# One tensor per chunk of tokens for the attention output, a third buffer for the reciprocals' rows, and a regrouped weight split

## The chip, the cores and the metric

The kernel runs on one core of a Trainium2 chip. The metric is the device time of one execution, in microseconds (us). Times of other kernels are set against it on the same chip.

## The reference, cut to what matters

The program is a chain of three layers over B·S = 2·768 = 1536 tokens of 512 features.

```python
# 1. attention of 8 heads of 64 features, with keys masked by equality of hash buckets
scores = np.where(mask, scale * q @ k.T, -1e9); attn = softmax(scores)   # sums + 1e-9
x = attn @ v                      # -> x: 1536 x 512
# 2. a gated dense layer
a = x @ w1; b = x @ w2            # 512 -> 1024 each
x = ((a * b) @ w3) @ w_out        # 1024 -> 1024 -> 512
# 3. a mixture of 8 experts, one per token, chosen by argmax of x @ w_gate + bias
out[mask] = gate_w * (np.maximum(x[mask] @ e1[e], 0) @ e2[e])
```

## The kernel before

**Storage.** The unnormalised attention output stands transposed, features on partitions: 512 features are four groups `hp` of 128 (two heads each), and tokens run along the free axis. There is one tensor for each of the two batches, `xT[b]` of `[P, HP, S + 1]` with S = 768; its last column holds a sum that is used for tokens without a matching key. The tokens are worked on in four chunks of CH = 384: chunks 0 and 1 are the halves of `xT[0]`, chunks 2 and 3 those of `xT[1]`.

**Splitting.** Matmuls take float32 numbers as a rounded high part and a remainder, in three products for each (`TERMS`: high·high, high·low, low·high). For the activations the high part is `x_t[ch]`, a tensor of its own, and the remainder `xlo` is written in place over the memory of `xT`.

**Normalisation of a chunk.** The attention output of each token and head is divided by its sum. The reciprocals come from DRAM (`rd`), spread over 64 partitions for each head by `load_r`, into the ring of buffers `rb`, two transfers for one `hp`. For chunks 1 to 3 `norm_step(ch, step)` starts one `hp` at each step: DVE makes `nw`, POOL multiplies `xT` by `rb` (L648) and adds `nw` (L649), ACT rounds it into `x_t` a step later (L651), and DVE writes the remainder a step after that (L653). Chunk 0 is normalised during attention, by DVE alone, in `norm_0`.

**The dense layer of a chunk.** `moe_f(ch, f)` computes 128 of the 1024 features in two tiles, `a` (j = 0) and `b` (j = 1), of 12 matmuls each (L686). ACT copies `a` to `asb` (L689), DVE multiplies it with `b` into `gf` (L696), ACT rounds that into `g` (L697), POOL subtracts the remainder (L698). In this phase the tiles turn over four PSUM buffers. The first four `f` of chunk 0 are worked in between the last attention steps, the last four after them.

**What runs when.** The order of the instructions on each engine is the order in which the code is written out. While chunk 0 does its `f` = 4 to 7, the steps of `norm_step(1, ·)` are issued, two ahead of each `moe_f`; while chunks 1 and 2 do `f` = 2 to 7, one step of the next chunk's normalisation follows each `moe_f`. The matrix products with `w3 @ w_out` (called w34; tiles `x2p`, L1022) of a chunk follow `f` = 3 of the next. `w34_prep` splits w34 in eight blocks at the start of chunk 1: ACT copies a block (L674), DVE subtracts (L675); the loaded w34 (`w34f`) shares its memory with the remainders. Waits between engines follow from the tensors that instructions touch: where two tensors lie on the same memory, as `xlo` on `xT`, a reader of the one is held by the last earlier writer of the other, whichever part it wrote.

**Transfers.** All loads named here are issued by SP, in the order of the code; an issue whose wait is open holds those behind it.

Of the kernel before, what the change touches and what calls it, by code (L numbers as in the profile page):

```python
# [8 lines left out]
F32 = mybir.dt.float32  # L9
# [11 lines left out]
P = 128  # L21
# [148 lines left out]
def body(tc, qT, kT, vP, w1d, w2d, w3d, wod, mod, wgate, mbias, e1, e2, cst, out):  # L170
# [6 lines left out]
    def one(name, shape, dt=F32, at_top=False):  # L177
        n = 4
        for d in shape[1:]:
            n *= d  # L180
        rings[name] = Ring(mem, name, n, 1, at_top)
        return rings[name](shape, dt)

    def ring(name, words, n, at_top=False, below=None):
        return Ring(mem, name, 4 * words, n, at_top, below)
# [26 lines left out]
    mv = one("mv", [P, B, HP])  # L212
    logit = one("logit", [P, TT, E])
    wgs = one("wgs", [P, 4, 32])
    mbs = one("mbs", [P, 2, E])
    mods = one("mods", [P, 2 * TT], I32)
    wgp = one("wgp", [P, 8, 32])
    xT = {b: one(f"xT{b}", [P, HP, S + 1]) for b in range(B)}

    rg = {"rb": ring("rb", CH, 2, True), "nw": ring("nw", CH, 1, True)}  # L220
    r_raw = ring("raw", S, 6, True)
    r_bt = ring("bt", S, 1, True)
    r_lo = ring("lo", S, 1, True)
# [164 lines left out]
    def stage_a(j):  # L388
        p, half, c = sunits[j]
        v = v_t[p]  # L390
        if c == 0:
            a_t[p, half] = ps("a", [P, HS + 1], f"a{p}_{half}")
        for hd in range(2):
            PE.matmul(  # L394
                a_t[p, half][64 * hd:64 * hd + 64, :], v[:, c, 64 * hd:64 * hd + 64], pts[j % NP][:, hd, :],
                start=(c == 0), stop=(c == QT - 1), tile_position=(0, 64 * hd),
            )
        if c == QT - 1:
            b, hp = divmod(p, HP)
            o = half * HS  # L400
            ACT.copy(xT[b][:, hp, o:o + HS + 1], a_t.pop((p, half)))

    def stage_n(p):
        b, hp = divmod(p, HP)
        sm = ps("m", [P, HS], f"n{p}")
        for half in range(2):
            acc = acc_t.pop((p, half))
            for hd in range(2):
                r = 64 * half + 32 * hd
                PE.matmul(  # L410
                    sm[r:r + 32, :], cs[:, 416:448], acc[:, hd, 0:HS], start=True, stop=True, tile_position=(0, r),
                )
        ss = r_ss([P, HS])
        ACT.copy(ss, sm)  # L414
        for half in range(2):
            SP.dma_start(sd[b, :, hp, half * HS:half * HS + HS], ss[64 * half:64 * half + 64:32, :])
        if hp == HP - 1:
            sm, r, z = (r_sr([P, 48]) for _ in range(3))
            SP.dma_start(sm, sd[b].rearrange("j h (a n) -> (j h a) n", n=48))

            def recip():
                DVE.tensor_scalar(r, sm, 1e-9, None, ALU.add)
                DVE.reciprocal(r, r)
                DVE.tensor_scalar(z, sm, 0.0, -4e9, ALU.is_equal, ALU.mult)
                DVE.tensor_add(r, r, z)
                SP.dma_start(rd[b].rearrange("j h (a n) -> (j h a) n", n=48), r)
                DVE.tensor_scalar(mv[:, b, :], xT[b][:, :, S], 1.0 / S, None, ALU.mult)

            late.append(recip)

# [204 lines left out]
        for j in range(2):  # L635
            SP.dma_start(rb_t[ch, hp][64 * j:64 * j + 64], rd[b, j, hp, o:o + CH].partition_broadcast(64))

    xlo = {b: mem.at(rings[f"xT{b}"].spans[0], [P, HP, S + 1], F32R, f"xlo{b}") for b in range(B)}

    def norm_x(ch, hp, part):  # L640
        b, o = divmod(ch * CH, S)
        if part and ch not in x_t:
            x_t[ch] = rg["x"]([P, HP, CH], F32R)
        x = xT[b][:, hp, o:o + CH]
        if part == 0:
            w = rg["nw"]([P, CH])
            DVE.tensor_scalar(w, rb_t[ch, hp], 0.0, mv[:, b, hp:hp + 1], ALU.is_lt, ALU.mult)
            POOL.tensor_mul(x, x, rb_t[ch, hp])  # L648
            POOL.tensor_add(x, x, w)  # L649
        elif part == 1:  # L650
            ACT.copy(x_t[ch][:, hp, :], x)  # L651
        else:
            DVE.tensor_sub(xlo[b][:, hp, o:o + CH], x, x_t[ch][:, hp, :].bitcast(F32))  # L653

    def norm_0(ch, hp, s):
        b, o = divmod(ch * CH, S)
        x = xT[b][:, hp, o:o + CH]
        if s == 0:
            DVE.tensor_mul(x, x, rb_t[ch, hp])
        elif s == 1:  # L660
            nw_t[ch, hp] = rg["nw"]([P, CH])
            DVE.tensor_scalar(nw_t[ch, hp], rb_t[ch, hp], 0.0, mv[:, b, hp:hp + 1], ALU.is_lt, ALU.mult)
        else:
            DVE.tensor_add(x, x, nw_t.pop((ch, hp)))
# [5 lines left out]

    TERMS = ((0, 0), (0, 1), (1, 0))

    def w34_prep(f):
        ACT.copy(w34[0][:, f, :], w34[2][:, f, :])  # L674
        DVE.tensor_sub(w34[1][:, f, :], w34[2][:, f, :], w34[0][:, f, :].bitcast(F32))  # L675

    ab_t, gspan = {}, []

    def moe_half(ch, f, j, tag="ab"):
        b, o = divmod(ch * CH, S)  # L680
        x = (x_t[ch], xlo[b][:, :, o:o + CH])
        fs = slice(f * P, f * P + P)
        t = ps(tag, [P, DM], f"ab{ch}{f}{j}")[:, 0:CH]
        for c in range(4):
            for i, (st, mv) in enumerate(TERMS):
                PE.matmul(t, w12[j][:, st, c, fs], x[mv][:, c, :], start=(c == 0 and i == 0), stop=(c == 3 and i == 2))  # L686
        if j == 0:
            ab_t[ch, f] = rg["asb"]([P, CH])
            ACT.copy(ab_t[ch, f], t)  # L689
            return  # L690
        if f % 4 == 0:
            gf_t[ch, f // 4] = rg["gf"]([P, 4, CH])
            g_t[ch, f // 4] = mem.at(gspan[GSPAN[ch][f // 4]], [P, 2, 4, CH], F32R, "g")
        gf = gf_t[ch, f // 4][:, f % 4, :]
        g = g_t[ch, f // 4][:, :, f % 4, :]
        DVE.tensor_mul(gf, ab_t.pop((ch, f)), t)  # L696
        ACT.copy(g[:, 0, :], gf)  # L697
        POOL.tensor_sub(g[:, 1, :], gf, g[:, 0, :].bitcast(F32))  # L698
# [91 lines left out]
    for i in range(NU + LEAD + NLAG + 1):  # L790
# [31 lines left out]
            norm_step(0, i - SWITCH - NSTEP)  # L822
        for ch, at in enumerate(NORM):
            for hp in range(HP):
                if i == at + (0, 0, 8, 11)[hp]:
                    load_r(ch, hp)
            if i == at + 4:
                for k in range(12):
                    after(k, lambda ch=ch, k=k: norm_0(ch, k // 3, k % 3))
# [8 lines left out]
        if done["n"] == 56 and len(rg["gf"].spans) == 1:  # L838
            r_st.close()
            rg["gf"].grow(1, 4 * 4 * CH)  # L840
            rg["rb"].grow(2, 4 * CH)
        p, ph = divmod(i, 12)
        j = i - LEAD + (i < SOON)
        both = grouped(i)
# [124 lines left out]
    load_r(1, 3)  # L969
    for f in range(0, 8, 2):  # L970
        SP.dma_start(w34[2][:, f:f + 2, :], w34d[f * P:(f + 2) * P, :].rearrange("(f p) n -> p f n", p=P))
    SP.dma_start(mbs, mbias.rearrange("m e -> (m e)").partition_broadcast(P))
    SP.dma_start(mods.bitcast(I64), mod)

# [61 lines left out]

    for ch in range(NCH):
        if ch == NCH - 1:
            rings["xT0"].close()
            gspan.append(mem.take(4 * 2 * 4 * CH))  # L1040
        for f in range(NEARLY if ch == 0 else 0, 8):
            if ch == 0:
                for step in range(2 * (f - NEARLY), 2 * (f - NEARLY) + 2):
                    norm_step(1, step)
            if ch == 1 and f < 3:
                for k in range(3 * f, min(8, 3 * f + 3)):
                    w34_prep(k)
            moe_f(ch, f)
            if f == 5:
                logit_mm(ch, 0)  # L1050
            if ch == 0 and f == 6:
                late.pop(0)()
            if ch and f == 1:
                logit_mm(ch - 1, 1)
                logit_evac(ch - 1)
            if ch and f == 2:
                logit_fin(ch - 1)
            if ch and ch + 1 < NCH:
                if f < HP:
                    load_r(ch + 1, f)  # L1060
                if 0 <= f - 2 < HP + 2:
                    norm_step(ch + 1, f - 2)
            if ch and f == 3:
                for tile in range(TC * (ch - 1), TC * ch - (ch == NCH - 1)):
                    for it in x2_items(tile):
                        it()
        if ch == 1:
            mf, mn = (one(n, [P, TT]) for n in ("mf", "mn"))
            b0, b1 = (one(n, [P, TT, E]) for n in ("b0", "b1"))
            DVE.tensor_copy(mf, mods.rearrange("p (t two) -> p t two", two=2)[:, :, 0])  # L1070
            DVE.tensor_scalar(mn, mf, -1.0, 1.0, ALU.mult, ALU.add)
            DVE.tensor_mul(b0, bc(mbs[:, 0, :], 1, TT), bc(mn, 2, E))
            DVE.tensor_mul(b1, bc(mbs[:, 1, :], 1, TT), bc(mf, 2, E))
            DVE.tensor_add(b0, b0, b1)
    for n in ("x", "rb", "nw", "asb"):
        rg[n].close()
    for n in ("xT1", "w0", "w1"):
        rings[n].close()
    xi = [it for tile in range(TT - 4, TT) for it in x2_items(tile)]
    for it in xi[:HOOKS[0]]:  # L1080
# [468 lines left out]
```

## Time and profile before

| | |
|---|---|
| time, median of 3 runs (lowest to highest) | 708.34 us (706.29 to 709.06) |
| profiled execution: its time | 704.57 us |
| profiled execution: span from first to last instruction | 702.2 us |
| mean granted TensorE clock | 0.983 |
| PE busy | 653.6 us, 93% of the span |
| DVE / ACT / POOL busy | 383.0 / 319.3 / 320.8 us |

The page and the views come from one execution. Durations are read from it; 2.4 us of its time lie outside the span, and its time is 0.5% below the median of the three runs. "Granted clock" 1.00 is TensorE's upper level (2.4 GHz), 0.50 the lower one (1.2 GHz). In a row, "[3.27 <-POOL xT L649]" says that the engine stood idle for 3.27 us before it and that the POOL instruction of line 649, which writes `xT`, ended that.

### The profile page before, as it was taken

How to read it: one execution, taken by the hardware profiler on the slowest of the kernel's cores; microseconds unless marked ns; L12 is line 12 of the kernel's file. 1: busy time of each engine (PE TensorE's matmuls, PEld its weight loads, DVE VectorE, ACT ScalarE, POOL GpSimd, SP SyncE). 2: the span in 40 equal slices, each digit the busy share in tenths (PEclk: the TensorE clock that was granted, in tenths of full speed). 3: DMA queues.
4: the chain of work that ended last, by engine and by line, in shares of the span. 5: the costliest groups of instructions: out<-in, count | busy, mean ns of one | idle time of the engine just before them, and what ended most of it. 6: DMA issues, size and time to landing. Idle time of an engine off the chain costs nothing. (4 is left out here: it accounts for less than half of the span.)

```text
span 702.2 us, 10151 instructions
## 1 busy us (share of the span) xinstructions
PE 653.6 (93%) x3650; PEld 516.7 (74%) x3650; DVE 383.0 (55%) x573; ACT 319.3 (45%) x510; POOL 320.8 (46%) x291
## 2 busy tenths in 40 slices
PE   7988999999999989976999979699999999999996
PEld 2644756666666645855998978598978998899884
DVE  6798777676867887521432311120176675665560
ACT  7466565656566447531332211121213665555551
POOL 7698986877778677752241330321114232011101
PEclk9999999999999999997999999899999999999999
DMA  8748372737565672203102001000007887766630
GB/s 228 232 136 224 101 245 86 230 114 191 178 166 175 165 214 79 100 25 121 48 15 64 12 0 46 0 1 16 16 17 257 291 297 237 233 208 215 210 136 18
DMA packets 40663, 93.88 MB, mean 134 GB/s; under 512 B 6544, under 2 KB 11008, under 8 KB 40608
## 3 DMA queue, kind: packets, MB, share of 16 engines
q1 hardware_dynamic: 38528, 86.62, 39.6%
q0 software_dynamic: 2080, 6.56, 2.8%
q8 instruction: 31, 0.51, 0.3%
q14 instruction: 24, 0.20, 0.1%
HBM read 72.98 MB, written 12.94 MB: 122 GB/s over the span
## 5 line engine op out<-in xcount | busy, mean ns | idle before, releaser
L686 PE MATMUL ab<-x,w 128*128 128x384 f32 x512 | 141.8, 353 | 0.6 <-ACT ss L414 0.6
L386 POOL TENSOR_TENSOR acc<-acc,pt 128x770 f32<-128x770 f32 x64 | 119.9, 1874 | 23.6 <-ACT pt L381 22.1
L356 DVE TENSOR_REDUCE nm<-m 128x1 f32<-128x768 f32 x96 | 91.4, 955 | 51.2 <-PE m L348 51.0
L381 ACT ACTIVATE pt<-s 128x768 f32<-128x768 f32 x96 | 77.9, 812 | 73.5 <-PE s L380 67.9
L686 PE MATMUL ab<-xlo,w 128*128 128x384 f32 x256 | 90.1, 352 | 20.6 <-POOL xT L649 20.6
L698 POOL TENSOR_TENSOR g<-gf,g 128x384 fp32r<-128x384 f32 x32 | 32.6, 1017 | 154.9 <-ACT g L697 153.6
L686 PEld LDWEIGHTS ab<-x,w 128*128 128x128 f32 x512 | 98.7, 199 | 5.8 <-issue 3.8
L380 PE MATMUL s<-q,k 128*128 128x384 f32 (+1 forms) x384 | 91.0, 359 | 4.0 <-ACT pt L381 3.9
L380 PEld LDWEIGHTS s<-q,k 128*128 128x128 f32 (+1 forms) x384 | 63.6, 189 | 38.7 <-issue 15.0
L1213 DVE TENSOR_TENSOR eu<-er,eu 128x1024 fp32r<-128x1024 f32 x56 | 67.6, 1223 | 23.7 <-ACT eu L1212 22.6
L696 DVE TENSOR_TENSOR gf<-asb,ab 128x384 f32<-128x384 f32 x32 | 17.7, 553 | 113.0 <-PE ab L686 113.0
L394 PE MATMUL a<-pt,v 128*64 128x385 f32 x384 | 74.5, 502 | 0.0
L1378 PE MATMUL e1F<-ex,eu 128*128 128x256 f32 x576 | 70.4, 283 | 0.5 <-DVE ex L1342 0.3
L1378 PEld LDWEIGHTS e1F<-ex,eu 128*128 128x128 f32 x576 | 69.9, 192 | 1.3 <-DVE ex L1342 0.5
L1404 POOL DMA_INDIRECT out<-o,sidx x13 | 14.2, 1095 | 122.3 <-ACT o L1403 106.2
L1396 PE MATMUL e2F<-eu,h 128*128 128x512 f32 x288 | 68.1, 392 | 0.0
L686 PEld LDWEIGHTS ab<-xlo,w 128*128 128x128 f32 x256 | 50.9, 199 | 22.1 <-POOL xT L649 22.0
L1212 ACT CAST eu<-er 128x1024 fp32r<-128x1024 f32 x56 | 57.6, 1047 | 8.8 <-DMA er<-e 8.8
L1396 PEld LDWEIGHTS e2F<-eu,h 128*128 128x128 f32 x288 | 53.2, 188 | 10.6
L348 PE MATMUL m<-k,q 78*128 78x384 f32 x192 | 52.5, 355 | 5.9 <-ACT pt L381 2.5
L1022 PE MATMUL x2p<-w,g 128*128 128x512 f32 x240 | 56.0, 391 | 0.0
L1022 PEld LDWEIGHTS x2p<-w,g 128*128 128x128 f32 x240 | 44.8, 188 | 9.6 <-issue 0.6
(207 smaller groups left out, 870.2 us busy)
## 6 DMA issues: line engine op xcount, KB each, us to landing
er<-e SPq DMA_DIRECT2D x56, 512.0 KB
cr<-w3d SPq DMA_DIRECT2D x16, 512.0 KB
cr<-wod SPq DMA_DIRECT2D x8, 512.0 KB
cr<-w1d SPq DMA_DIRECT2D x8, 512.0 KB
wfd<-cT SPq DMA_DIRECT2D x16, 256.0 KB
cr<-w2d SPq DMA_DIRECT2D x8, 512.0 KB
st<-wfd SPq DMA_DIRECT2D x16, 256.0 KB
raw<-kT SPq DMA_DIRECT2D x8, 384.0 KB
```

Of the source, the lines that this page charges most:

```text
L348: PE.matmul(s[:, half, 0:HS], q[0:KROWS[hd], 0, qt * P:qt * P + P], k[0:KROWS[hd], 0, half * HS:half * HS + HS], start=True, stop=True,)
L356: DVE.tensor_reduce(nm[:, at:at + 1], s[:, :, 0:HS], AX.XY, ALU.max, negate=True)
L380: PE.matmul(s[:, hd, 0:HS], k[0:n, i, c * P:c * P + P], q[0:n, i, cl], start=(i == 0), stop=(i == 1))
L381: ACT.activation(pts[j % NP][:, :, 0:HS], s[:, :, 0:HS], AF.Exp, scale=SCALE)
L386: POOL.tensor_add(acc, pts[(j - 1) % NP] if c == 1 else acc, pts[j % NP])
L394: PE.matmul(a_t[p, half][64 * hd:64 * hd + 64, :], v[:, c, 64 * hd:64 * hd + 64], pts[j % NP][:, hd, :], start=(c == 0), stop=(c == QT - 1 ...
L686: PE.matmul(t, w12[j][:, st, c, fs], x[mv][:, c, :], start=(c == 0 and i == 0), stop=(c == 3 and i == 2))
L1022: PE.matmul(st["ps"], g_t[ch, f // 4][:, a, f % 4, i * P:i * P + P], w34[b][:, f, :], start=(f == 0 and k == 0), stop=(f == 7 and k == 2),)
L1212: ACT.copy(t[:, 0, sl], raw)
L1213: DVE.tensor_sub(t[:, 1, sl], raw, t[:, 0, sl].bitcast(F32))
L1378: PE.matmul(o[f], w[:, st, c, fs], x[:, mv, c, :], start=(c == 0 and i == 0), stop=(c == 3 and i == 2))
L1396: PE.matmul(o, h[:, st, f, sl], w[:, mv, f, :], start=(f == 0 and k == 0), stop=(f == 7 and k == 2))
```

## The change

The attention output is kept in four tensors `xT[ch]` of `[P, HP, CH + 1]`, one for each chunk, and `xlo` in four over them. The ring `rb` has three buffers from the start in place of two, and four after it grows, as before; the loads of `hp` 2 and 3 of chunk 0 are issued eight and three slots earlier. `w34_prep` takes a group of blocks, copies all of it and then subtracts all of it. `mbs` and `mods`, two small tables, get their memory later in the program; their loads stay at their place.

```diff
-    mbs = one("mbs", [P, 2, E])
-    mods = one("mods", [P, 2 * TT], I32)
...
-    xT = {b: one(f"xT{b}", [P, HP, S + 1]) for b in range(B)}
-
-    rg = {"rb": ring("rb", CH, 2, True), "nw": ring("nw", CH, 1, True)}
+    xT = [one(f"xT{ch}", [P, HP, CH + 1]) for ch in range(NCH)]
+
+    rg = {"rb": ring("rb", CH, 3, True), "nw": ring("nw", CH, 1, True)}
...
-            o = half * HS
-            ACT.copy(xT[b][:, hp, o:o + HS + 1], a_t.pop((p, half)))
+            ACT.copy(xT[2 * b + half][:, hp, :], a_t.pop((p, half)))
...
-    xlo = {b: mem.at(rings[f"xT{b}"].spans[0], [P, HP, S + 1], F32R, f"xlo{b}") for b in range(B)}
+    xlo = [mem.at(rings[f"xT{ch}"].spans[0], [P, HP, CH + 1], F32R, f"xlo{ch}") for ch in range(NCH)]
...
-        x = xT[b][:, hp, o:o + CH]
+        x = xT[ch][:, hp, 0:CH]
...
-            DVE.tensor_sub(xlo[b][:, hp, o:o + CH], x, x_t[ch][:, hp, :].bitcast(F32))
+            DVE.tensor_sub(xlo[ch][:, hp, 0:CH], x, x_t[ch][:, hp, :].bitcast(F32))
...
-    def w34_prep(f):
-        ACT.copy(w34[0][:, f, :], w34[2][:, f, :])
-        DVE.tensor_sub(w34[1][:, f, :], w34[2][:, f, :], w34[0][:, f, :].bitcast(F32))
+    def w34_prep(fs):
+        for f in fs:
+            ACT.copy(w34[0][:, f, :], w34[2][:, f, :])
+        for f in fs:
+            DVE.tensor_sub(w34[1][:, f, :], w34[2][:, f, :], w34[0][:, f, :].bitcast(F32))
...
-        x = (x_t[ch], xlo[b][:, :, o:o + CH])
+        x = (x_t[ch], xlo[ch][:, :, 0:CH])
...
-                if i == at + (0, 0, 8, 11)[hp]:
+                if i == at + (0, 0, 0, 8)[hp]:
                     load_r(ch, hp)
...
-            rg["rb"].grow(2, 4 * CH)
+            rg["rb"].grow(1, 4 * CH)
+            rg["rb"].i = 7
...
+    mbs = one("mbs", [P, 2, E])
+    mods = one("mods", [P, 2 * TT], I32)
     SP.dma_start(mbs, mbias.rearrange("m e -> (m e)").partition_broadcast(P))
...
-            rings["xT0"].close()
+            for n in ("xT0", "xT1"):
+                rings[n].close()
...
-                for k in range(3 * f, min(8, 3 * f + 3)):
-                    w34_prep(k)
+                w34_prep(range(3 * f, min(8, 3 * f + 3)))
...
-    for n in ("xT1", "w0", "w1"):
+    for n in ("xT2", "xT3", "w0", "w1"):
```

The order of instructions on PE, DVE, ACT and POOL is the same before and after; on SP one pair of loads moves. What changes on the four engines is which instructions wait, and on whom. A row below is one instruction (or xN alike): its line, operation, what it writes and reads, its shape, and the engines or transfers that it waits for.

PE, at the first tile after attention, `ab040` (chunk 0, `f` = 4, j = 0); `x_` is the high part, `xlo0` the remainder. Before:

```order
L686 MATMUL ab040_2936<-x_223_2554,w0_220_2500 128x384 [waits Activation_49]
L686 MATMUL ab040_2936<-xlo0_27_96,w0_220_2500 128x384 [waits Pool_49]
L686 MATMUL ab040_2936<-x_223_2554,w0_220_2500 128x384 x2
L686 MATMUL ab040_2936<-xlo0_27_96,w0_220_2500 128x384
L686 MATMUL ab040_2936<-x_223_2554,w0_220_2500 128x384 x2
```

After:

```order
L684 MATMUL ab040_2940<-x_225_2556,w0_222_2502 128x384 [waits Activation_49]
L684 MATMUL ab040_2940<-xlo0_27_96,w0_222_2502 128x384
L684 MATMUL ab040_2940<-x_225_2556,w0_222_2502 128x384 x2
L684 MATMUL ab040_2940<-xlo0_27_96,w0_222_2502 128x384
L684 MATMUL ab040_2940<-x_225_2556,w0_222_2502 128x384 x2
```

The second matmul waits for POOL before and for nobody after. The same wait goes from the tiles `ab050`, `ab230`, `ab240`, `ab250` and `ab260`.

PE, at the first tile of chunk 1 (`ab100`), which reads the remainders `xlo1` in the kernel after. Before:

```order
L686 MATMUL ab100_3094<-xlo0_27_96,w0_220_2500 128x384
L686 MATMUL ab100_3094<-x_256_2930,w0_220_2500 128x384 x2
L686 MATMUL ab100_3094<-xlo0_27_96,w0_220_2500 128x384
L686 MATMUL ab100_3094<-x_256_2930,w0_220_2500 128x384 x2
L686 MATMUL ab100_3094<-xlo0_27_96,w0_220_2500 128x384 [waits DVE_49]
```

After:

```order
L684 MATMUL ab100_3098<-xlo1_28_97,w0_222_2502 128x384 [waits Pool_49]
L684 MATMUL ab100_3098<-x_260_2934,w0_222_2502 128x384 x2
L684 MATMUL ab100_3098<-xlo1_28_97,w0_222_2502 128x384
L684 MATMUL ab100_3098<-x_260_2934,w0_222_2502 128x384 x2
L684 MATMUL ab100_3098<-xlo1_28_97,w0_222_2502 128x384 [waits DVE_49]
```

Here a wait for POOL is new: it is for the last write of POOL to the tensor of this chunk. Chunks 2 and 3 begin with the same wait after; before, chunk 2 did.

SP, in attention slot 74, where the reciprocals' rows of chunk 0 are loaded (`rb`; `cr` are weights, `wfd` a store of weights). Before:

```order
L636 DMA rb_182_2039<-rd_60 64x384 [waits DMAHW1_49]
L636 DMA rb_182_2039<-rd_60 64x384 [waits DMAHW2_49]
L466 DMA cr_184_2069<-w2d 128x512 [waits DMAHW3_49,DVE_49]
L515 DMA wfd_58<-cT_183_2047 128x512 [waits DMAHW4_49,DVE_49]
L466 DMA cr_187_2116<-w2d 128x512 [waits DMAHW5_49]
```

After:

```order
L633 DMA rb_184_2041<-rd_60 64x384 [waits DMAHW1_49]
L633 DMA rb_184_2041<-rd_60 64x384 [waits DMAHW2_49]
L633 DMA rb_185_2044<-rd_60 64x384 [waits DMAHW3_49]
L633 DMA rb_185_2044<-rd_60 64x384 [waits DMAHW4_49]
L463 DMA cr_187_2074<-w2d 128x512 [waits DMAHW5_49,DVE_49]
```

The two loads of `hp` 2 have moved to here from a place some 20 issues later, ahead of a load and a store of weights and of the moves of the next pair of heads.

## Rows read from the trace of the kernel before

**Rows 1.** PE's waits, whole span: total us, times, longest.

```profile
PE ab L686 <- POOL xT L649: 20.6, 5, 6.5
```

**Rows 2.** PE's timeline, the five matmuls after these waits: start, duration.

```profile
313.23 0.44 PE L686 MATMUL ab<-xlo,w 128*128 128x384 f32 x1 [3.27 <-POOL xT L649]
...
325.80 0.69 PE L686 MATMUL ab<-xlo,w 128*128 128x384 f32 x1 [6.54 <-POOL xT L649]
...
411.52 0.44 PE L686 MATMUL ab<-xlo,w 128*128 128x384 f32 x1 [3.85 <-POOL xT L649]
...
442.12 0.44 PE L686 MATMUL ab<-xlo,w 128*128 128x384 f32 x1 [3.98 <-POOL xT L649]
...
452.07 0.44 PE L686 MATMUL ab<-xlo,w 128*128 128x384 f32 x1 [2.98 <-POOL xT L649]
```

**Rows 3.** Windows: length, busy PE PEld DVE ACT POOL, clock, DMA share, GB/s.

```profile
313.23:316.97 3.74, 3.74 (x13) 3.74 (x14) 0.00 (x0) 0.03 (x1) 0.00 (x0) 0.55 0.51 157
325.80:330.72 4.92, 4.92 (x16) 4.92 (x16) 0.00 (x0) 0.48 (x1) 0.00 (x0) 0.51 0.02 3
330.72:407.67 76.95, 76.95 (x432) 70.33 (x431) 25.07 (x48) 20.73 (x42) 20.69 (x21) 1.00 0.10 32
412.50:416.32 3.82, 3.82 (x14) 3.82 (x14) 0.00 (x0) 0.48 (x1) 0.00 (x0) 0.55 0.00 0
442.90:446.94 4.04, 4.04 (x17) 4.04 (x16) 0.00 (x0) 0.48 (x1) 0.00 (x0) 0.58 0.00 0
452.85:456.88 4.03, 4.03 (x17) 4.03 (x16) 0.00 (x0) 0.48 (x1) 0.00 (x0) 0.58 0.00 0
457.00:542.89 85.89, 85.89 (x490) 76.71 (x488) 30.61 (x98) 17.87 (x33) 18.33 (x18) 1.00 0.17 58
```

**Rows 4.** Timeline of chunk 0 after attention, all engines: start, duration, idle before.

```profile
309.52 0.44 PE L686 MATMUL ab<-x,w 128*128 128x384 f32 x1 [0.60 <-ACT ss L414]
...
312.19 0.99 POOL L649 TENSOR_TENSOR xT<-xT,nw 128x384 f32<-128x384 f32 x1
...
319.19 0.55 DVE L696 TENSOR_TENSOR gf<-asb,ab 128x384 f32<-128x384 f32 x1 [11.02 <-PE ab L686]
...
324.88 0.86 POOL L649 TENSOR_TENSOR xT<-xT,nw 128x384 f32<-128x384 f32 x1
...
332.86 0.55 DVE L653 TENSOR_TENSOR xlo<-xT,x 128x384 fp32r<-128x384 f32 x1
...
335.43 0.48 ACT L689 COPY asb<-ab 128x384 f32<-128x384 f32 x1 [1.47 <-PE ab L686]
...
339.59 0.48 ACT L689 COPY asb<-ab 128x384 f32<-128x384 f32 x1 [0.96 <-PE ab L686]
```

**Rows 5.** POOL's timeline, `f` = 5 of chunk 2: the last add of chunk 3.

```profile
449.23 1.03 POOL L698 TENSOR_TENSOR g<-gf,g 128x384 fp32r<-128x384 f32 x1 [7.17 <-ACT g L697]
...
451.16 0.86 POOL L649 TENSOR_TENSOR xT<-xT,nw 128x384 f32<-128x384 f32 x1
```

**Rows 6.** Timeline of the split of w34 in chunk 1.

```profile
342.87 1.02 POOL L698 TENSOR_TENSOR g<-gf,g 128x384 fp32r<-128x384 f32 x1 [3.14 <-ACT g L697]
343.34 1.09 DVE L675 TENSOR_TENSOR w<-w34f,w 128x512 fp32r<-128x512 f32 x1 [1.10 <-ACT w L674]
344.47 0.62 ACT L674 CAST w<-w34f 128x512 fp32r<-128x512 f32 x1 [1.16 <-DVE w L675]
...
350.54 0.69 DVE L675 TENSOR_TENSOR w<-w34f,w 128x512 fp32r<-128x512 f32 x1 [0.69 <-ACT w L674]
350.61 0.19 PEld L686 LDWEIGHTS ab<-x,w 128*128 128x128 f32 x1 [0.63 <-ACT w L674]
```

**Rows 7.** Timelines of SP and DVE: loads of `rb` for chunk 0, the wait.

```profile
209.16 2.42 SPq L636 DMA_DIRECT2D rb<-rd  x4
...
239.02 1.25 SPq L636 DMA_DIRECT2D rb<-rd  x2
...
245.47 0.56 DVE L659 TENSOR_TENSOR xT<-xT,rb 128x384 f32<-128x384 f32 x1 [1.86 <-DMA rb<-rd]
```

More of the change, by code (lines that the diff above doesn't have):

```diff
@@ L426, in recip @@
                 SP.dma_start(rd[b].rearrange("j h (a n) -> (j h a) n", n=48), r)
-                DVE.tensor_scalar(mv[:, b, :], xT[b][:, :, S], 1.0 / S, None, ALU.mult)
+                DVE.tensor_scalar(mv[:, b, :], xT[2 * b + 1][:, :, CH], 1.0 / S, None, ALU.mult)
             late.append(recip)
@@ L652, in norm_x @@
         else:
-            DVE.tensor_sub(xlo[b][:, hp, o:o + CH], x, x_t[ch][:, hp, :].bitcast(F32))
+            DVE.tensor_sub(xlo[ch][:, hp, 0:CH], x, x_t[ch][:, hp, :].bitcast(F32))
     def norm_0(ch, hp, s):
-        b, o = divmod(ch * CH, S)
-        x = xT[b][:, hp, o:o + CH]
+        b = ch * CH // S
+        x = xT[ch][:, hp, 0:CH]
         if s == 0:
@@ L671, in body @@
     TERMS = ((0, 0), (0, 1), (1, 0))
-    def w34_prep(f):
-        ACT.copy(w34[0][:, f, :], w34[2][:, f, :])
-        DVE.tensor_sub(w34[1][:, f, :], w34[2][:, f, :], w34[0][:, f, :].bitcast(F32))
+    def w34_prep(fs):
[3 more added lines that the diff above has]
+            DVE.tensor_sub(w34[1][:, f, :], w34[2][:, f, :], w34[0][:, f, :].bitcast(F32))
     ab_t, gspan = {}, []
     def moe_half(ch, f, j, tag="ab"):
-        b, o = divmod(ch * CH, S)
-        x = (x_t[ch], xlo[b][:, :, o:o + CH])
+        x = (x_t[ch], xlo[ch][:, :, 0:CH])
         fs = slice(f * P, f * P + P)
```

## The prediction

> **What bounds the kernel now.** I read the busy shares first: PE works 93% of the span, so a gain has to come out of PE's idle time or out of work done at a low clock. PE's own waits come next. Among them one stands out: five waits, 20.6 us together, of products that read `xlo` for POOL's add into `xT` [rows 1]. No other single wait of PE is over 5 us in sum. The timeline shows where the five stand: two in chunk 0 (3.27 and 6.54 us) and three in chunk 2 (3.85, 3.98 and 2.98 us) [rows 2]. The reader should see what is odd in them: a product of chunk 0 needs remainders of chunk 0, and these were finished long before; POOL at that moment writes chunk 1. Chunks 0 and 1 share a tensor, as do 2 and 3. Chunk 1 and chunk 2 do not share one, and that is the test the profile offers without any change: while PE works on chunk 1, POOL normalises chunk 2 by the same steps, and PE is busy for 76.95 of 76.95 us [rows 3].
>
> The windows then give what such a wait costs besides its length. PE resumes, and within about a us its granted clock stands at the lower level for some 4 us, in all five places: 0.55, 0.51, 0.55, 0.58, 0.58 over 3.74, 4.92, 3.82, 4.04 and 4.03 us [rows 3]. Where PE is not interrupted the clock stays at 1.00, for 85.89 us on end in the longest window I took [rows 3].
>
> **Part by part: the four tensors.** The order of instructions on PE, DVE, ACT and POOL stays; the waits of `ab040`, `ab050`, `ab230` to `ab260` for POOL go. Removed are
>
> - the waits: 3.27 + 6.54 + 3.85 + 3.98 + 2.98 = 20.62 us;
> - the low clock behind them: time at clock c does c of its length in full-rate work, so each window loses (1 − c) of itself: 3.74·0.45 + 4.92·0.49 + 3.82·0.45 + 4.04·0.42 + 4.03·0.42 = 1.68 + 2.41 + 1.72 + 1.70 + 1.69 = 9.20 us.
>
> Together 29.8 us. All of it lies on PE, which has nothing else to do meanwhile, and what follows (chunks, then routing and experts) is released by PE or by what PE feeds, so I take it as coming off the end.
>
> The question is what is late next. The new wait is at the first tile of chunk 1, for the last add of chunk 1's normalisation. In chunk 0 I follow the timeline. `f` = 4 starts at 309.52 as before, since that wait is for ACT [rows 4]. One `f` at the full clock takes 339.59 − 335.43 = 4.16 us, from one `asb` copy to the next [rows 4]. So `f` = 4 ends near 313.7, and four `f` with some 1.1 us of logit products end near 327.3; before, the same point was near 341.3. The normalisation: the second `hp` is done at 312.19 + 0.99 = 313.2, unchanged. DVE can form `gf` of `f` = 4 near 313.9 in place of 319.19. From that `gf` to the end of the add for the fourth `hp` the chain took 324.88 + 0.86 − 319.19 = 6.55 us [rows 4], through DVE, ACT and POOL and with no PE in it; so it ends near 320.5. Two roundings on ACT and two subtractions of 0.55 us on DVE remain [rows 4], near 322.5. Chunk 1 starts 5 us later. Meanwhile ACT's copy of the `f` = 5 tile is late, near 319, but PE has four PSUM buffers, which is two `f` or 8.3 us, and it asks for that buffer again only near 323. I count nothing for it; without that cover it would cost up to 3 us.
>
> In chunk 2 the last add follows POOL's `g` of `f` = 5, which starts at 449.23, and ends at 451.16 + 0.86 = 452.02 [rows 5]. PE, already in `f` = 6, had stood 2.98 us for it [rows 2]. `f` = 6 and 7 are 8.3 us of work, so the slack there is 5.3 us. The very last subtraction of a chunk waits for the last `gf` before and after alike, and at the boundary of chunks 1 and 2 the window shows PE without idle time [rows 3].
>
> **The rest of the change.** The third `rb` buffer and the earlier loads: DVE stood 1.86 us for the load of the third `hp`, issued at 239.02; it now goes out behind the four issues at 209.16 [rows 7]. PE was not released by that instruction, so I take 0, bounds 1.86 us of gain (all of DVE's wait reaches PE) and 1.25 us of loss (two more issues, by their own row, hold up a load that somebody waits for) [rows 7]. The regrouped split: ACT no longer stands for DVE, 1.16 us in the row shown, and DVE's first subtraction waits for two more copies of 0.62 us [rows 6]. PE's weight load waited 0.63 us for ACT at 350.61 [rows 6], while its matmuls were not idle; hidden by the four PSUM buffers, I take 0, bounds 0.63 us of gain and 1.24 us of loss. `mbs` and `mods` are loaded at the same place of the queue, and only their address changes: 0.
>
> A rule that speaks against the four tensors bears on the chain above. The row: one subtraction of DVE with two SBUF operands took 1.09 us where the same form takes 0.69, and it ended 0.54 us after POOL's subtraction, which ran until 343.89 [rows 6]. So the two engines hold each other up, and in the changed kernel they are pressed closer together. The Trainium skill, page "SBUF — State Buffer", section "SBUF: two separate sides", says that VectorE and GpSimd share one pair of ports as an exclusive lock, and the one that comes second stands still for the other's whole instruction; the trace agrees. By the row an encounter costs 0.40 us; at worst, a full POOL instruction of 1.02 us [rows 6]. DVE has four such subtractions in chunk 0's chain: 1.6 to 4.1 us, within the slack of 5. By either the sum stays at 29.8.
>
> **The sum.** 702.2 − 29.8 = 672.4 us of span; with the 2.4 us around it 674.8, against 704.57 of the profiled execution. That execution lies 0.5% below the median of the three runs; 708.34 · 674.8 / 704.57 = 678.4. I predict 678 us.
>
> **Rivals.**
>
> 1. *The chain of normalisation becomes late.* The ports' lock, or POOL's order (`g` of one `f` stands between the adds), stretches the chain past the 5 us of slack in chunk 0 or the 5.3 in chunk 2, and PE waits at the start of chunk 1 or 3. For it: `ab100` now waits for POOL, and the busy shares of DVE and POOL in these 15 us rise. Against it: the same steps run beside chunk 1 without a gap [rows 3]. Price: a wait as long as the largest of today's with its low clock, 6.54 + 2.41 = 9 us back, 687 us; half of that is 683.
> 2. *The waits only move.* The remainders still lie over the tensor that POOL writes, so the wait could come back whole within the chunk. It would be so if the products of a chunk ran while POOL writes that same chunk. They do not: POOL's last add of a chunk is 5 us or more ahead of its first product. No change, 706 to 710 us.
> 3. *Slower: the second weight product's load.* Chunk 1 starts 14 us earlier, and the first thing ACT does there is to copy `w34f`; behind it stands the `asb` copy that frees PE's buffers. If that load had not landed, ACT would stand, and PE 8.3 us later. To turn 29.8 us into a loss of more than 0.5% (3.5 us), it would have to land 29.8 + 3.5 + 8.3 = 41.6 us after 327.3, at 369. Against it: in the window from 325.80 the transfers are at 0.02 of their time [rows 3], so the load had landed by then. Its price at that point is 712 us.
> 4. *The clock is not given back.* PE then has some 200 us without a wait ahead of the experts. If such a stretch were granted the lower level for 18 us, 9.2 us would be lost again: 688 us. Against it: 76.95 and 85.89 us at 1.00 [rows 3].
>
> **How the numbers follow.** The forecast gets 0.80, rival 1 0.12, rival 2 0.03, rival 3 0.01, rival 4 0.03, and 0.01 for what I have not thought of, slower. A measurement of this kernel tells about 0.5%, 3.5 us, from no change. Faster by more: 0.80 + 0.12 + 0.03 = 0.95; same 0.03; slower 0.02. The forecast's own range is 674 to 682: gains of 1.86 + 0.63 and losses of 1.25 + 1.24 around 678.4, and about 1.5 for the spread of runs. For 8 in 10 with part of rival 1, and with the profiled execution's lower level in mind (674.8 less 2.5 is 672), I give 672 to 687.
>
> **What would show it.** Right: no wait of PE for POOL of over 0.5 us between 300 and 480; the granted clock 1.00 there; mean clock above 0.99; chunk 1's first product near 327 and the split of w34 with three ACT copies in a row; DVE's wait for `rb` gone; 0.60 us for ACT still there at 309. Wrong: PE idle at the first tiles of chunks 1 and 3, with POOL or DVE named; ACT standing at the first copy of `w34f` for a transfer; PE idle on `ab` tiles for ACT's `asb` copies in chunk 0, which would mean that the four buffers do not cover the chain; or PE's waits gone and the end of the span less than 25 us earlier, in which case the time went to a later stage.

## The result, and the profile after

| | before | after |
|---|---|---|
| median, lowest to highest of 6 runs | 706.24 us (704.08 to 709.06) | 673.44 us (673.09 to 673.76) |
| profiled execution: time, span | 704.57, 702.2 us | 673.39, 671.3 us |
| granted clock, mean | 0.983 | 0.998 |

The ratio is 0.953, with a 95% interval of 0.951 to 0.956. The kernel became 4.7% faster; 678 us was forecast, with a range of 672 to 687.

The page of the changed kernel begins so (span; busy time, share and instructions of each engine; then PE's busy share and granted clock in tenths, in 40 slices of the span; below, its two groups of `ab` matmuls with busy us and mean ns, and the idle time before them):

```profile
span 671.3 us, 10130 instructions
...
PE 644.8 (96%) x3650; PEld 507.9 (76%) x3650; DVE 383.0 (57%) x573; ACT 319.4 (48%) x510; POOL 320.8 (48%) x291
...
PE   7998999999999999999999999999999999999995
...
PEclk9999999999999999999999999999999999999999
...
L684 PE MATMUL ab<-x,w 128*128 128x384 f32 x512 | 135.3, 339 | 0.6 <-ACT ss L411 0.6
...
L684 PE MATMUL ab<-xlo,w 128*128 128x384 f32 x256 | 86.4, 338 | 0.0
```

DVE, ACT and POOL do the same work as before. PE's busy time fell by 8.8 us (653.6 to 644.8) although it runs the same 3650 matmuls: I read that as the low clock that went (9.2 us were forecast). The rest of the gain is idle time of PE that went. PE's waits in the changed kernel, longest sums first (total us, times, longest):

```profile
PE zk L768 <- DVE cs L738: 4.5, 1, 4.5
PE s L378 <- ACT pt L379: 3.8, 8, 0.6
PE m L346 <- DVE nm L354: 2.8, 6, 0.8
...
PE m L346 <- ACT pt L379: 0.6, 1, 0.6
PE ab L684 <- ACT ss L411: 0.6, 1, 0.6
```

The wait of [rows 1] is not there any more, in any size. The windows over chunk 0's last four `f`, chunk 1, chunk 2, the first part of chunk 3, and all of it, answer to [rows 3] (columns as there):

```profile
307.69:325.70 18.01, 18.01 (x105) 17.14 (x106) 6.87 (x14) 5.28 (x11) 10.57 (x11) 1.00 0.47 143
325.70:378.00 52.30, 52.30 (x282) 47.24 (x281) 14.43 (x28) 14.77 (x31) 15.59 (x16) 1.00 0.15 46
378.00:430.70 52.70, 52.70 (x286) 47.65 (x285) 11.28 (x26) 10.93 (x23) 15.54 (x16) 1.00 0.04 16
430.70:477.00 46.30, 46.30 (x258) 42.35 (x257) 6.48 (x13) 8.71 (x18) 8.13 (x8) 1.00 0.03 12
307.69:477.00 169.31, 169.31 (x925) 154.38 (x926) 39.06 (x81) 39.68 (x83) 49.82 (x51) 1.00 0.12 38
```

For 169.31 us PE is never idle and never at the lower level. The timeline of chunk 0, all engines, in order of time (start, duration, idle before), answers to [rows 4]:

```profile
307.69 0.45 PE L684 MATMUL ab<-x,w 128*128 128x384 f32 x1 [0.60 <-ACT ss L411]
...
312.28 0.56 DVE L694 TENSOR_TENSOR gf<-asb,ab 128x384 f32<-128x384 f32 x1 [5.96 <-PE ab L684]
...
313.83 0.86 DVE L644 TENSOR_SCALAR nw<-rb,mv 128x384 f32<-128x384 f32 x1 [0.53 <-DMA rb<-rd]
...
318.09 0.86 POOL L646 TENSOR_TENSOR xT<-xT,nw 128x384 f32<-128x384 f32 x1
...
319.10 1.32 POOL L696 TENSOR_TENSOR g<-gf,g 128x384 fp32r<-128x384 f32 x1
...
320.00 0.47 ACT L687 COPY asb<-ab 128x384 f32<-128x384 f32 x1
...
320.13 0.71 DVE L650 TENSOR_TENSOR xlo<-xT,x 128x384 fp32r<-128x384 f32 x1 [0.58 <-ACT x L648]
```

`f` = 4 starts 1.83 us earlier than in [rows 4] (307.69 against 309.52): something was gained in attention. The last subtraction for chunk 1 ends at 320.84, and chunk 1 starts at 325.7, 4.9 us later (327.3 was forecast, from a start of `f` = 4 at 309.52; 1.83 earlier that is 325.5). DVE now stands 0.53 us for the `rb` rows of chunk 1's third `hp`, which costs PE nothing. From the first `gf` to the end of the last add the chain takes 318.95 − 312.28 = 6.67 us (6.55 forecast). In chunk 2, POOL's last add for chunk 3 answers to [rows 5]:

```profile
425.06 0.86 POOL L646 TENSOR_TENSOR xT<-xT,nw 128x384 f32<-128x384 f32 x1
```

It ends at 425.92, 4.8 us ahead of chunk 3. The regrouped split in chunk 1 answers to [rows 6], ACT's and DVE's timelines:

```profile
326.87 1.66 ACT L672 CAST w<-w34f 128x512 fp32r<-128x512 f32 x3
...
328.56 2.14 DVE L674 TENSOR_TENSOR w<-w34f,w 128x512 fp32r<-128x512 f32 x3 [2.15 <-ACT w L672]
```

ACT copies three blocks without a stop. Three subtractions take 2.14 us, 0.71 us each on average, where [rows 6] has one of 1.09. SP's loads answer to [rows 7]: six issues in a row, and DVE's wait of 1.86 us is gone.

```profile
208.97 3.71 SPq L633 DMA_DIRECT2D rb<-rd  x6
...
238.70 1.24 SPq L633 DMA_DIRECT2D rb<-rd  x2
```

So the span shrank by 702.2 − 671.3 = 30.9 us: 1.83 ahead of `f` = 4, and 29.07 behind it.

### The profile page after: what moved, and what is told of

Same layout as the page of the kernel before. It is cut to its first block, busy times and chain, and to the rows that moved or that the text cites. A ratio compares the mean times of both kernels' runs of the same rounds, so it can differ in the third digit from the quotient of the medians.

```text
span 671.3 us, 10130 instructions
## 1 busy us (share of the span) xinstructions
PE 644.8 (96%) x3650; PEld 507.9 (76%) x3650; DVE 383.0 (57%) x573; ACT 319.4 (48%) x510; POOL 320.8 (48%) x291
## 5 line engine op out<-in xcount | busy, mean ns | idle before, releaser
L684 PE MATMUL ab<-x,w 128*128 128x384 f32 x512 | 135.3, 339 | 0.6 <-ACT ss L411 0.6
L684 PEld LDWEIGHTS ab<-x,w 128*128 128x128 f32 x512 | 93.4, 188 | 5.8 <-issue 4.4
L684 PE MATMUL ab<-xlo,w 128*128 128x384 f32 x256 | 86.4, 338 | 0.0
L1023 PE MATMUL x2p<-w,g 128*128 128x512 f32 x240 | 57.4, 396 | 0.0
L1023 PEld LDWEIGHTS x2p<-w,g 128*128 128x128 f32 x240 | 44.8, 188 | 10.8 <-issue 0.6
L599 PE MATMUL w<-wo,w 128*128 128x512 f32 x192 | 49.0, 393 | 0.4 <-POOL w L494 0.4
```

The costliest lines, as they stand in the source:

```text
L1023: PE.matmul(st["ps"], g_t[ch, f // 4][:, a, f % 4, i * P:i * P + P], w34[b][:, f, :], start=(f == 0 and k == 0), stop=(f == 7 and k == 2),)
```

## The experiments

**The theory.** T: five waits come from tensors shared by two chunks; each costs its length and a stretch at the low clock behind it, and nothing else becomes late. The rivals are that the waits would return elsewhere, and that the low clock would be spent elsewhere. A question beside it is which of the other edits brings the 1.83 us ahead of `f` = 4. Kernels named together below ran on one chip, beside runs of the kernel before.

### One batch at a time

The kernel before, with `xT` split for one batch alone; everything else, the loads and the split of w34 included, stays (`xN` names the tensors):

```diff
-    xT = {b: one(f"xT{b}", [P, HP, S + 1]) for b in range(B)}
+    PARTED = (1, 0)          # batch0; (0, 1) is batch1
+    xT, xO, xN = {}, {}, {}
+    for b in range(B):
+        for h in range(2):
+            if h == 0 or PARTED[b]:
+                xN[2 * b + h] = f"xT{2 * b + h}"
+                xT[2 * b + h] = one(xN[2 * b + h], [P, HP, (CH if PARTED[b] else S) + 1])
+            else:
+                xT[2 * b + 1], xN[2 * b + 1] = xT[2 * b], xN[2 * b]
...
```

Expected of batch0: 

> The kernel before, with only the first batch's tensor split into one for each chunk; loads and weight split are left as they were before. Theory (the five waits of PE come from a tensor shared by two chunks, and each costs its length and the low clock behind it): the waits in chunk 0 go and those in chunk 2 stay, 3.27 + 6.54 + 1.68 + 2.41 = 13.9 us less than the kernel before, so about 692.6 beside 706.5. Rival 1 (a wait only moves to a later place of the same chain): 705 to 708. Rival 2 (the low clock is lost elsewhere all the same): 9.8 us less, 696.7.

Expected of batch1: 

> The kernel before, with only the second batch's tensor split into one for each chunk; the rest is left. Theory: the waits in chunk 2 go and those in chunk 0 stay, 3.85 + 3.98 + 2.98 + 1.72 + 1.70 + 1.69 = 15.9 us less than the kernel before, so about 690.6 beside 706.5; the gains of this kernel and of the one with the first batch's split add up to 29.8 us. Rival 1 (the waits only move): 705 to 708. Rival 2 (the low clock is lost elsewhere all the same): 10.8 us less, 695.7.

Measured: batch0 691.13 us (689.69 to 694.6), ratio 0.981 [0.976, 0.985]; batch1 690.76 us (687.66 to 692.38), ratio 0.977 [0.973, 0.982]; before 705.74 us. By the ratios that is 13.7 us [10.6, 16.7] and 15.9 us [13.0, 19.0] less, where T said 13.9 and 15.9; together 29.6, where it said 29.8. An agreement to 0.2 us is luck with intervals of 3 us to either side. But the prices without the clock, 9.8 for batch0 and 10.8 for batch1, lie outside their intervals. PE's waits for POOL, batch0 first, then batch1:

```profile
PE ab L701 <- POOL xT L664: 10.8, 3, 4.0
```

```profile
PE ab L701 <- POOL xT L664: 9.8, 2, 6.5
```

In each kernel the waits of the batch that still shares its tensor stand as in [rows 2], to 0.02 us, and those of the other are gone. The windows where they were, batch0 from `f` = 4 on and batch1 over chunks 1 and 2 (columns as in [rows 3]), show PE busy throughout at the upper level:

```profile
308.98:390.00 81.02, 81.02 (x452) 74.52 (x453) 27.37 (x52) 23.11 (x47) 29.00 (x30) 1.00 0.19 62
```

```profile
336.00:480.00 144.00, 144.00 (x777) 131.38 (x778) 35.45 (x72) 33.73 (x70) 38.19 (x39) 1.00 0.08 25
```

T holds for these five waits: they do not move, and the low clock is not lost elsewhere in these stretches.

### How much slack the chain has

The changed kernel, with 4 or 12 extra copies on POOL that leave the values as they are:

```diff
+            if (ch, hp) == (1, 3):
+                for _ in range(4):          # pool12: 12
+                    POOL.tensor_copy(x, x)
```

Expected of pool4: 

> The changed kernel, with four more copies by POOL of 128x384 elements in place, between the last add of the normalisation of chunk 1 and what POOL does next; they leave the values as they are. At some 0.9 us for each copy the chain of chunk 1 ends some 3.6 us later, near 324.5, and chunk 1's first product starts near 325.7. Theory (slack of 5 us covers it): no change, 673.5 within 0.7. Rival (the slack is not there, since PE would wait for POOL's next remainder of g or for PSUM): 675 to 679 with PE idle in chunk 0 or at the start of chunk 1.

Expected of pool12: 

> The changed kernel, with twelve more copies by POOL at the same place, some 10.8 us, which leave the values as they are. Theory (slack of 5 us, and each wait of PE is followed by a stretch at the low clock): PE waits 5 to 7 us for POOL at the first product of chunk 1, and loses 1.7 to 2.4 us more behind it: 680 to 682.5. Rival 1 (no price of the clock): 678.5 to 680.5 with the granted clock at 1.00 behind the wait. Rival 2 (DVE stands still beside POOL, so that the chain grows by more than POOL's own work): over 684.

Measured: pool4 673.48 us (673.18 to 673.99), no new wait of PE; pool12 677.91 us (676.59 to 678.66). A copy takes 0.56 us, not the 0.9 I had estimated from other POOL rows, so the chain was stretched by 2.2 and 6.8 us. The sizes expected of pool12 are too high for that reason: with 6.8 us and a slack of 5, PE would wait 1.8 us. It waited 2.37, at the place expected, the first product of chunk 1, but not for the engine expected. Timeline of pool12, all engines:

```profile
319.08 6.78 POOL L649 COPY xT<-xT 128x384 f32<-128x384 f32 x12
...
325.90 1.33 DVE L653 TENSOR_TENSOR xlo<-xT,x 128x384 fp32r<-128x384 f32 x1 [7.36 <-POOL xT L649]
...
327.26 0.51 ACT L651 CAST x<-xT 128x384 fp32r<-128x384 f32 x1 [8.17 <-DVE xlo L653]
...
327.68 0.47 ACT L690 COPY asb<-ab 128x384 f32<-128x384 f32 x1
...
328.21 0.69 PE L687 MATMUL ab<-x,w 128*128 128x384 f32 x1 [2.37 <-ACT asb L690]
```

Read it from below. PE waits 2.37 us at the first matmul of chunk 1, not for POOL's write to chunk 1's tensor but for a PSUM buffer, which ACT frees by its copy of `f` = 6 into `asb`; that copy stands on ACT behind the rounding of the last `hp`; the rounding waits for DVE, and DVE for POOL. The copy into `asb` is 7.68 us later than in the changed kernel (327.68 against 320.00) and PE waited 2.37, so the cover was 5.3 us. The window behind the wait:

```profile
328.21:332.20 3.99, 3.99 (x14) 3.99 (x15) 2.78 (x8) 1.58 (x4) 1.52 (x2) 0.58 0.03 6
```

It loses 3.99 · 0.42 = 1.68 us. 2.37 + 1.68 = 4.05 us, and the span is 4.0 us longer than the 671.3 of the changed kernel. So in this execution the price of the clock is there, against rival 1, and the time of rival 2, over 684, is far off; what DVE lost beside POOL is 0.77 us of the chain (1.33 in place of 0.56). The price need not be paid each time: one of the four executions took 676.59 us at a mean clock of 0.999, where the other three, at 0.996, took 677.9 to 678.7. There is more in the rows: the rounding of the last `hp` reads a part of `xT` that the DVE row above it does not write. The two touch one tensor, and the one waits for the other. The sharing that the change removed between chunks goes on between the `hp` of one chunk; it is hidden there.

### The regrouped split

oldsplit is the changed kernel with the block-by-block split of w34 of the kernel before; again is the changed kernel itself, on the same chip.

```diff
-                w34_prep(range(3 * f, min(8, 3 * f + 3)))
+                for k in range(3 * f, min(8, 3 * f + 3)):
+                    w34_prep(k)          # ACT copies one block, DVE subtracts it
```

Expected of oldsplit: 

> The kernel after, with the split of w34 block by block as before. The prediction's theory: hidden by four PSUM buffers, 673.4 us within 0.6, with ACT's waits for DVE of 1.16 us back in the rows. Rival: the chunk starts 14 us earlier and the cover has become thinner, so that ACT's waits reach PE: 1.2 to 3.7 us more (the idle time that the grouping took from ACT in its three groups), 674.6 to 677.

Expected of again: 

> The kernel after once more, on the chip and in the rounds of the other three, so that differences of 1 us can be read: 673.4 us, within 0.5.

Measured: oldsplit 673.04 us (672.84 to 675.0), again 673.52 us (673.3 to 673.82). ACT's copies in oldsplit (busy us, mean ns, idle before):

```profile
L671 ACT CAST w<-w34f 128x512 fp32r<-128x512 f32 x8 | 5.0, 619 | 5.0 <-DVE w L672 5.0
```

ACT's 5.0 us of standing are back, and no new wait of PE is there: the edit is worth nothing that these runs can tell, as forecast.

### What the loads bring, first try

oldloads is the changed kernel with two `rb` buffers and the old slots; lateloads has the third and fourth `hp` a slot later still:

```diff
-    rg = {"rb": ring("rb", CH, 3, True), "nw": ring("nw", CH, 1, True)}
+    rg = {"rb": ring("rb", CH, 2, True), "nw": ring("nw", CH, 1, True)}
...
-                if i == at + (0, 0, 0, 8)[hp]:
+                if i == at + (0, 0, 8, 11)[hp]:          # lateloads: (0, 0, 9, 12)
```

Expected of oldloads: 

> The kernel after, with the reciprocals' loads and the ring of two buffers as before. Two theories for the 1.8 us by which attention ends earlier in the kernel after (PE starts f = 4 of chunk 0 at 307.69 in place of 309.52). Data: DVE no longer stands 1.86 us for the load of the third hp. Buffers: where two score tiles of the last pair of heads (slots 90 and 91) wait for DVE in the kernel after, they wait for ACT here, as before, and PE stands 0.96 us twice. Both expect 675.2 us, 1.8 above the kernel after (673.4); the rival that the loads are worth nothing expects 673.4.

Expected of lateloads: 

> The same, with the loads of the third and fourth hp one slot later than before. Here the two score tiles take the PSUM buffers as in the kernel after (they wait for DVE), while the data come later than in the kernel before. The theory of buffers expects 673.4 us, as the kernel after, with DVE's wait for the load longer than the 1.86 us of before and PE without the two waits of 0.96 us. The theory of data expects 675.2 us or more.

Measured: oldloads 674.78 us (674.63 to 674.91), lateloads 674.41 us (674.15 to 674.45), beside the 673.52 of again. In oldloads PE waits twice in the last pair of heads, ahead of score tiles `m`:

```profile
258.77 0.62 PE L346 MATMUL m<-k,q 78*128 78x384 f32 x2 [0.96 <-ACT pt L379]
...
262.69 0.62 PE L346 MATMUL m<-k,q 128*128 128x384 f32 x2 [0.96 <-ACT pt L379]
```

The kernel before has the same two waits. Of the changed kernel only the second is left, at 0.28 us, for DVE. The kernel before first, then the changed one:

```profile
259.06 0.62 PE L348 MATMUL m<-k,q 78*128 78x384 f32 x2 [0.96 <-ACT pt L381]
...
262.99 0.61 PE L348 MATMUL m<-k,q 128*128 128x384 f32 x2 [0.96 <-ACT pt L381]
```

```profile
260.95 0.62 PE L346 MATMUL m<-k,q 128*128 128x384 f32 x2 [0.28 <-DVE nm L354]
```

That is 1.92 − 0.28 = 1.64 us, and `f` = 4 starts 1.67 us later in oldloads than in again (309.45 against 307.78). lateloads is without them, but there DVE waits 3.09 us for `rb`, and PE has a new wait, whose cause was not followed:

```profile
248.61 0.62 PE L346 MATMUL m<-k,q 78*128 78x384 f32 x2 [1.44 <-ACT pt L379]
```

So lateloads fits neither side (673.4 and 675.2 were expected): it changed more than one thing at once, and decides nothing.

### What the loads bring, second try

Which PSUM buffer a tile gets depends on the order of the program, transfers included, and the slot of one load is enough to change it: in the program of l811, below, the first of the two score tiles lies in PSUM bank 4, in that of l810 in bank 6, where the changed kernel has it. l811 and l810 are the changed kernel, three buffers and all, with the old slot 8 for the third `hp`; they differ by one slot of the fourth:

```diff
-                if i == at + (0, 0, 0, 8)[hp]:
+                if i == at + (0, 0, 8, 11)[hp]:          # l810: (0, 0, 8, 10)
```

The first of the two score tiles, as it stands in PE's order, with whom it waits for, l811 first, then l810:

```text
L346 MATMUL m_3_0_2504<-k_18_87,q_16_85 128x384 [waits DMAHW7_49,Activation_49]
L346 MATMUL m_3_0_2504<-k_18_87,q_16_85 128x384 [waits DMAHW7_49,DVE_49]
```

Expected of l811: 

> The changed kernel (three buffers for rb) with the loads of chunk 0 at their old slots, 8 and 11 for the third and fourth hp. The program then gives the two first score tiles of the last pair of heads PSUM buffers that ACT's exponentials free, as in the kernel before. Both theories (buffers; earlier data) expect 674.8 within 0.3, chunk 0's f = 4 starting near 309.4, and two waits of PE of 0.96 us for ACT between 257 and 263.

Expected of l810: 

> The same, but the fourth hp's load one slot earlier (8 and 10), which changes by itself which PSUM buffers those two score tiles get: they are then freed by DVE, as in the changed kernel, while the third hp's rows come as late as in the kernel with 8 and 11. Theory A (the loads edit gains by the PSUM buffers that it happens to change): 673.5 within 0.3, the two waits of 0.96 us gone, f = 4 starting near 307.8. Theory B (it gains because the rows of the third hp arrive earlier): 674.8, f = 4 starting near 309.4, whatever the waits do. In between: some of either.

Measured: l810 672.80 us (672.71 to 673.34), l811 676.03 us (674.68 to 676.71); the ratios to before are 0.954 [0.952, 0.957] and 0.958 [0.955, 0.961]. In l810 the two waits of 0.96 us are gone and `f` = 4 starts at 307.52, while DVE still waits for the rows of the third `hp`:

```profile
244.73 0.97 DVE L656 TENSOR_TENSOR xT<-xT,rb 128x384 f32<-128x384 f32 x1 [1.36 <-DMA rb<-rd]
```

Theory A holds: the gain comes from the buffers, and earlier rows bring nothing. l811 was expected at 674.8; two of its five runs are there, and three between 676.0 and 676.7. The window behind its first wait of 0.96 us, and behind that of oldloads, which has the same work there:

```profile
258.71:263.12 4.41, 4.41 (x14) 2.02 (x14) 1.93 (x4) 0.00 (x0) 2.81 (x5) 0.63 0.35 110
```

```profile
258.77:261.73 2.96, 2.96 (x14) 1.43 (x14) 1.94 (x4) 0.00 (x0) 2.73 (x5) 1.00 0.26 93
```

In the one the clock fell, in the other it did not: 4.41 us against 2.96 for the same 14 matmuls. That accounts for 1.45 us of the profiled execution of l811 (676.03 us, at a mean clock of 0.994). It does not account for its slowest run, 676.71 us at 0.998; that one stays open. Why one slot of a load changes which buffers are handed out was not followed further.

### The two cheapest forms together

best is the changed kernel with the loads of l810 and the split of oldsplit; again2 is the changed kernel, on the same chip.

```diff
-                if i == at + (0, 0, 0, 8)[hp]:
+                if i == at + (0, 0, 8, 10)[hp]:
...
-                w34_prep(range(3 * f, min(8, 3 * f + 3)))
+                for k in range(3 * f, min(8, 3 * f + 3)):
+                    w34_prep(k)
```

Expected of best: 

> The changed kernel with two of its edits replaced by what the runs liked best: loads of chunk 0's rows at slots 8 and 10 for the third and fourth hp (672.8 on another chip), and the split of w34 block by block as before (673.0 on another chip). If both differences are real and add: 672.3 to 672.6, 1 us below the changed kernel. If they are differences of chips: 673.5, the same as the changed kernel within 0.3. In both cases no wait of PE for POOL's writes to xT and no wait of 0.96 us for the buffers.

Expected of again2: 

> The changed kernel once more, on the chip of the next run: 673.5 within 0.3.

Measured: best 672.98 us (672.74 to 673.28), again2 673.24 us (673.0 to 673.85). The ranges overlap and the medians are 0.26 us apart: the same. So the lower medians of l810 and oldsplit are no gain that can be told from what runs and chips differ by.

## Why the prediction was right, and where it was off

**The waits and their clock (20.62 + 9.20 = 29.82 us): right.** Behind the start of `f` = 4 the kernel gained 29.07 us. The two batches apart gave 13.7 and 15.9. The test that the profile offered beforehand, chunk 1 against chunk 2 [rows 3], told truly what separate tensors would do.

**The next thing to be late: the slack was right, what takes it first was wrong.** The prediction had 5 us of slack in chunk 0 and 5.3 in chunk 2; the trace shows 4.9 and 4.8, and pool12 found 5.3 before PE stands. But what is late first is not POOL's last add, for which `ab100` waits. It is the copy into `asb` that frees a PSUM buffer for that tile, where the prediction counted nothing because of the four buffers. The size of the slack came out right for another wait than the one it was worked out for; that is partly luck. Rival 1 did not come.

**The ports' lock: too dear.** I allowed 1.6 to 4.1 us for four subtractions of DVE beside POOL. They took 0.55, 0.56, 0.56 and 0.71 us, so the encounters cost these four some 0.2 us. POOL can be the one that is held: its subtraction at 319.10 started 0.11 us after a subtraction of DVE and took 1.32 us, where 1.0 is usual. None of it reached PE. The hold-up itself is real: in pool12 the subtraction at 325.90 took 1.33 us beside a POOL instruction of 0.99 that had started 0.08 us earlier, 0.77 more than alone. The Trainium skill, page "SBUF — State Buffer", section "SBUF: two separate sides", has the second of two such instructions wait for the whole of the first; this row agrees in the main: 0.91 us of the POOL instruction were left, and DVE lost 0.77.

**The third buffer and the loads (0, bounds +1.86 and −1.25): mis-sized.** They gained 1.83 us at the start of `f` = 4; in time it is 1.26 us by oldloads, and 3.2 by l811 against l810, of which 1.9 are the two waits and most of the rest, in the profiled execution, is the low clock behind the first of them (1.45). The upper bound held the first two numbers, not the third, and its reason was wrong: not DVE's wait for `rb`, which in l810 is there at no cost, but two waits of PE for PSUM buffers that the order of the loads happens to hand out.

**The split of w34 (0): right**, by oldsplit. `mbs` and `mods` were not tried apart.

**The scaling to the median: the step that failed.** On the profiled execution the forecast was 674.8, and 673.39 came: 1.83 gained in attention, 0.75 missing from the waits, 0.3 less around the span. To reach 678 I multiplied by 708.34/704.57, as if the 3.8 us by which that median lies above the profiled execution would stay in proportion; this adds 3.6 us to the forecast. More than half of that came from the three runs known then: over six runs the median before is 706.24, 1.7 us above the profiled execution. The rest did not stay either, since the surplus is not spread over the program. In nine runs of before beside l810, five at a granted clock of 0.983 took 703.8 to 704.5 us, three at 0.978 took 705.9 to 706.4, and one at 0.974 took 708.5; beside the other experiments it is much the same, and the twelve runs at 0.983 are the twelve fastest of 32. The surplus goes with the clock. I take it to be longer or additional low stretches behind PE's waits, of which l811 shows one; no slow execution of the kernel before was profiled, so this is not shown. In the changed kernel the surplus is gone: its runs spread over 0.7 us, those of before over 5. The forecast that should have stood is 674.8. The forecast's own range, 674 to 682, does not hold the 673.44 us; the wider one, from 672, does, because its lower end was set with the level of the profiled execution in mind.

**Rivals 2, 3 and 4** are excluded by the windows and timelines above: no wait moved, ACT's first copy of `w34f` (326.87) waits for nothing, and the clock stays at 1.00 for the whole 169 us.

## What to carry to other kernels

When PE waits for a writer that works on data of another stage, look at which tensor the two share; another stage that shares none is a ready-made test, and splitting the tensor by stage removed the waits here, with their low clock. A median that lies above a profiled execution is not a factor for a forecast: see first whether the surplus follows the granted clock, and whether the change removes the waits behind it. When an edit of transfers moves the time, look at what it did to the order in which buffers are handed out before believing in earlier data.

## What the runs showed that I had not expected

- A short wait can bring a low stretch. Behind 0.96 us of waiting, l811 ran 4.41 us at 0.63, and batch1 the same tiles 4.57 us at 0.63; oldloads, in its profiled execution, ran them at 1.00. PE had stood twice for 0.5 to 0.6 us in the seven us ahead of it, in all of them.
- The price behind a wait is not fixed either. batch1's wait of 6.55 us at 328.21 has 7.79 us at 0.62 behind it, which lose 2.96 us, where the kernel before lost 2.41 behind the same wait [rows 3]:

```profile
328.21:336.00 7.79, 7.79 (x32) 6.92 (x32) 0.70 (x2) 0.59 (x2) 0.00 (x0) 0.62 0.01 2
```

- An in-place copy of 128x384 on POOL took 0.56 us, where its adds and multiplications of that shape take 0.86 to 1.02.
